# First network in units of 1, 2, 3, 4 and 6 tiles, with a re-ordered attention on fixed PSUM banks

## The chip, the core and the metric

The kernel runs on one core of a Trainium2 chip. The metric is the time of one execution on the device in microseconds (us); the median of three runs of the kernel before is 1231.76 us (1231.2 to 1231.81). TensorE does the matmuls, VectorE and ScalarE everything elementwise, SyncE starts nearly all the transfers.

## What is computed

```python
kv  = einsum('bhsd,bhse->bhde', k, v)            # 4 batches, 8 heads, 576 tokens, width 64
out = einsum('bhsd,bhde->bhse', q, kv)
x   = out / sqrt(mean(out * out, -1) + 1e-06) * g_norm     # then 2304 tokens x 512
h   = x @ w_in                                   # first network, 2048 columns
x   = (h * clip(h + 3, 0, 6) / 6) @ w_out
p   = domain_probs / domain_probs.sum(-1)        # second network, 4 experts of 1024 columns
out = sum over e of p[:, e] * (max(x @ w1[e], 0) @ w2[e])
```

The weights of the first network arrive as 64-bit floats and are converted in the kernel.

## The kernel before, in words

**Attention (L169 to L322, loop at L461).** It is cut into eight parts i, half a batch (four heads) each. Four steps belong to a part. `att_q` transposes q by a matmul with the identity into `pq` and, for the last ninth of the tokens, into `kvp`; ScalarE copies both to `qT` (L217, L219). `att_kv` multiplies k and v into `kvp` and ScalarE copies the result to `kvbd` (L234). `att_out` multiplies `qT` and `kvbd` into three PSUM tiles `po` (L247), ScalarE squares them (L253), and VectorE sums the squares into `ssq` (L256); `att_rms` makes the factor `ri` of it in six small VectorE instructions and a ScalarE square root (L277 to L286) and multiplies `po` by it into `xt` (L269, three instructions, called the scaling of part i below). `att_x` transposes `xt` back into `px` (L305), ScalarE copies that to `xh` (L315) and VectorE makes the rest `xl` (L316): `xh + xl` is the input of the first network in two terms. Round i of the loop holds `att_q` and `att_kv` of part i, `att_out` of part i-1, `att_x` of part i-2.

**First network (L329 to L396).** The 2048 columns are 16 tiles of 128. Tiles are grouped in units; for every unit the five blocks of tokens (four of 512, one of 256) are gone through, and for every block the tiles of the unit. One such step is an item: `ff_in` has 12 matmuls of 512 columns into `ph`, then ScalarE and VectorE make `gH` and `gL` (L340 to L343), and three items later `ff_out` has 12 matmuls into four PSUM banks (L357). At the end of a block in a unit, the four banks are copied to `acc` by ScalarE (first unit, L371) or added to it by VectorE (other units, L373). The first four items' `ff_in` are in a list `EARLY` and are issued inside the attention by `fill`.

**Conversion (L130 to L162).** A tile has two halves, w_in and w_out. A half takes three ScalarE instructions (L142, L143, L158) and seven of VectorE (L145 to L160), all of 512 columns. Below, the halves are numbered in the order in which they are converted. `conv(k)` asks for k steps of them in the attention, `pull` (L408) for steps by a budget during the items, and only so far ahead as L413 and L415 allow.

**Order.** The program is not executed in the order in which it is written: a list scheduler places the instructions of each engine and mixes neighbouring steps, conversions above all. The resulting order is fixed before the run. The second network (L509 on) is not touched by the change.

Of the kernel before, what the change touches and what calls it, by code (L numbers as in the profile page):

```python
# [17 lines left out]
def kernel(  # L18
# [34 lines left out]
    UNITS1 = (2, 4, 4, 6)  # L53
# [7 lines left out]
    NA = NW - UNITS1[0]  # L61
    LAG = 3
    FMAX = 3.0e38
# [18 lines left out]
    psb = ctx.enter_context(tc.tile_pool(name="psb", bufs=5, space=bass.MemoryType.PSUM))  # L82
    psc = ctx.enter_context(tc.tile_pool(name="psc", bufs=1, space=bass.MemoryType.PSUM))

    turn = [0]

    def bank_b(shape, name):
        turn[0] += 1
        pool, tag = (psc, "c") if turn[0] % 6 == 0 else (psb, "b")
        return pool.tile(shape, F32, tag=tag, name=name)  # L90
# [4 lines left out]
    three = const.tile([P, 1], F32, name="three")  # L95
    gcol = const.tile([P, 1], F32, name="gcol")
# [33 lines left out]
    def convert(n):  # L130

        u, f = ftiles[n]
        w = wp.tile([P, 2, 2, KD * P], F32R, tag=f"w{(NA + n) % NW}", name="w")
        W[u, f] = w
# [28 lines left out]


# [38 lines left out]
    def att_q(i):  # L203
# [5 lines left out]
        t["kvp"] = kvp = [bank_b([P, 2, D], "kvp") for _ in range(NP)]  # L209
        for j in range(CJ):  # L210
            for x in range(2):
                for r in range(NP):
                    to = pq[r][half[x ^ r], j, :] if j < CB else kvp[r][half[x ^ r], 1, :]
                    nc.tensor.matmul(  # L214
                        to, lhsT=t["q"][half[x], r, j, :], rhs=ident[half[x], half[x]], start=True, stop=True)
        for r in range(NP):
            nc.scalar.activation(out=qv[:, r, :, :CB], in_=pq[r].rearrange("p j s -> p s j"), func=AF.Copy)  # L217
        for r in range(NP):
            nc.scalar.activation(out=qv[:, r, :, CB], in_=kvp[r][:, 1, :], func=AF.Copy)  # L219

    def att_kv(i):
# [4 lines left out]
        for j in range(CJ):  # L226
            for x in range(2):
                for r in range(NP):
                    nc.tensor.matmul(  # L229
                        kvp[r][half[x ^ r], 0, :], lhsT=t["k"][half[x], r, j, :], rhs=t["v"][half[x], r, j, :],  # L230
                        start=(j == 0), stop=(j == CJ - 1))
        for r in range(NP):
            for x in range(2):
                nc.scalar.activation(  # L234
                    out=kvbd[i % 2][half[x ^ r], r, half[x]], in_=kvp[r][half[x ^ r], 0, :], func=AF.Copy)

    def att_out(i):
# [5 lines left out]
        for tt in banks(b):  # L243
            po = psb.tile([P, 2, NP, P], F32, tag="b", name="po")
# [14 lines left out]
    def att_rms(i):  # L259
# [4 lines left out]
        va, r0, w1_, ri = (sp.tile([P, 5, HH], F32, tag=n, name=n) for n in ("va", "r0", "nw", "ri"))  # L264

        def scale():
            for g, tt in enumerate(banks(b)):
# [8 lines left out]
        return [  # L276
            lambda: nc.vector.tensor_scalar(  # L277
                out=va, in0=ssq, scalar1=1.0 / D, scalar2=1e-6, op0=ALU.mult, op1=ALU.add),
            lambda: nc.scalar.activation(out=r0, in_=va, func=AF.Sqrt),
            lambda: nc.vector.reciprocal(out=r0, in_=r0),  # L280
            lambda: nc.vector.scalar_tensor_tensor(
                out=w1_, in0=va, scalar=FMAX, in1=r0, op0=ALU.min, op1=ALU.mult),
            lambda: nc.vector.tensor_tensor(out=w1_, in0=w1_, in1=r0, op=ALU.mult),
            lambda: nc.vector.tensor_scalar(
                out=w1_, in0=w1_, scalar1=-0.5, scalar2=1.5, op0=ALU.mult, op1=ALU.add),
            lambda: nc.vector.tensor_tensor(out=ri, in0=w1_, in1=r0, op=ALU.mult),  # L286
# [3 lines left out]
    def att_x(i):  # L290
# [8 lines left out]
        def bank(rs, o0, o1):  # L299
            px = psb.tile([P, len(rs), o1 - o0], F32, tag="b", name="px")  # L300
# [18 lines left out]
        for r in range(NP):  # L319
            bank([r], *long)  # L320
        bank(list(range(NP)), *short)
# [56 lines left out]
    EARLY = [(0, t, f) for f in range(UF[0]) for t in range(2)]  # L378
    nearly = [0]

    def fill():
        ff_in(*EARLY[nearly[0]])
        nearly[0] += 1

    def step(n):
# [39 lines left out]

    def conv(k):
        for _ in range(k):
            if cv[0] >= UF[0]:
                return
            if cv[1] is None:  # L430
                cv[1] = convert(cv[0])
            if next(cv[1], None) is None:
                cv[0], cv[1] = cv[0] + 1, None

# [3 lines left out]
    zp = psb.tile([P, DM], F32, tag="b", name="zp")  # L438
# [9 lines left out]
    load_raw()  # L448
    load_raw()
# [4 lines left out]
    nc.gpsimd.memset(three, 3.0)  # L454

# [4 lines left out]
    conv(5)  # L460
    for i in range(NHB + 2):  # L461
        if 1 <= i < NHB - 1:
            att_load(i + 1)
        if i == 4:
            nc.sync.dma_start(out=dp, in_=moe2_domain_probs.rearrange("(t p) e -> p t e", p=P))
        if i < NHB:
# [7 lines left out]
        rms = []  # L474
        if 0 <= i - 1 < NHB:
            att_out(i - 1)
            rms = att_rms(i - 1)
            rms.pop(0)()
        em = att_x(i - 2) if i >= 2 else []
        if i == NHB:  # L480
            fill()

        order = ([em[0][0]] if em else []) + rms[:1] + [x for x, _ in em[1:]]
        los = [x for _, x in em]
        order += los[:1] + rms[1:2] + los[1:2] + rms[2:4] + los[2:3] + rms[4:]
        for x in order:
            x()
    while nearly[0] < len(EARLY):
        fill()

    N3 = start[NU1 - 1, 0] + 3 * UF[NU1 - 1]
    for n in range(NI):
        step(n)
        if n == 8:
# [299 lines left out]
```

## Time and profile before

| | |
|---|---|
| median of three runs | 1231.76 us |
| the profiled execution | 1232.57 us |
| its span, first to last instruction | 1230.8 us |
| TensorE, share of the span | 99% |
| VectorE, ScalarE | 62%, 47% |
| mean granted TensorE clock | 0.993 |

The profiled execution is 0.81 us above the median, and 1.77 us of it lie outside its span. Shares are averages over the whole span: the attention takes its first 99 us, the first network goes on to about 480 us, the second takes the rest.

### The profile page before, as it was taken

What the parts mean: (1) busy time and instruction counts of PE and PEld (TensorE: products, weight loads), DVE (VectorE), ACT (ScalarE), POOL (GpSimd) and SP (SyncE); (2) the same over time, 40 slices, a digit from 0 to 9 for tenths busy, and PEclk for the clock granted to TensorE, in tenths of its full rate; (3) what the DMA queues carried; (4) which work ended last, traced back from release to release, by engine and by line L of the source; (5) the groups of instructions that cost most, each with busy time, mean ns of one, the idle gap of its engine ahead of it and who ended that gap; (6) DMA issues with size and microseconds to landing.
All of it is one profiled execution on the core that took longest, in us unless ns stands there. A gap on an engine that the chain in (4) does not pass through costs nothing.

```text
span 1230.8 us, 17514 instructions
## 1 busy us (share of the span) xinstructions
PE 1213.0 (99%) x7069; PEld 1067.4 (87%) x7069; DVE 759.0 (62%) x1457; ACT 574.6 (47%) x1146; POOL 1.6 (0%) x12
## 2 busy tenths in 40 slices
PE   7999999999999999999999999999999999999998
PEld 5778888888888889999999989999999899999997
DVE  6879993794533655565656576656565866565643
ACT  6667742542422434444444455444444644444442
POOL 0000000000000000000000000000000000000000
PEclk8999999999999999999999999999999999999999
DMA  9802320120010002222122222212222221112101
GB/s 359 258 22 69 104 86 1 52 69 1 26 44 1 1 1 69 69 69 69 69 69 69 69 86 103 69 69 69 69 69 69 73 98 64 66 66 66 68 34 52
DMA packets 60833, 87.15 MB, mean 71 GB/s; under 512 B 5200, under 2 KB 37968, under 8 KB 60752
## 3 DMA queue, kind: packets, MB, share of 16 engines
q1 hardware_dynamic: 60592, 86.03, 20.7%
q8 instruction: 55, 0.90, 0.3%
q14 instruction: 26, 0.21, 0.1%
q10 hardware_dynamic: 160, 0.00, 0.0%
HBM read 81.30 MB, written 4.72 MB: 70 GB/s over the span
## 4 chain that ended last, share of the span: by engine, by line
PE 94%; DVE 3%; DMA 2%; ACT 1%; issue 0%
PE po L636 30%; PE po L357 16%; PE qa L662 14%; PE qb L662 14%; PE ph L334 5%; PE ph L335 5%; PE ph L336 5%; PE po L247 1%; PE kvp L229 1%; DVE acc L652 1%; DMA qin<-in_q_dram 1%; DVE xs L550 1%; PE px L305 1%; DMA kin<-in_k_dram 1%; DVE st L609 1%; PE pq L214 0%
## 5 line engine op out<-in xcount | busy, mean ns | idle before, releaser
L636 PE MATMUL po<-wout,g 128*128 128x512 f32 x1728 | 402.0, 390 | 0.0
L636 PEld LDWEIGHTS po<-wout,g 128*128 128x128 f32 x1728 | 323.6, 188 | 65.4
L662 PE MATMUL qb<-xs,win 128*128 128x384 f32 x1008 | 203.4, 336 | 1.2 <-ACT us L702 1.2
L662 PE MATMUL qa<-xs,win 128*128 128x384 f32 x1008 | 203.2, 336 | 0.1
L357 PE MATMUL po<-gH,w 128*128 128x512 f32 (+1 forms) x640 | 193.7, 368 | 0.0
L549 ACT ACTIVATE wout<-raw 128x512 fp32r<-128x512 f32 x96 | 55.4, 624 | 275.4 <-PE po L636 275.4
L662 PEld LDWEIGHTS qb<-xs,win 128*128 128x128 f32 x1008 | 178.1, 188 | 3.8 <-ACT us L702 1.8
L662 PEld LDWEIGHTS qa<-xs,win 128*128 128x128 f32 x1008 | 178.2, 188 | 2.7 <-ACT st L698 0.4
L550 DVE TENSOR_TENSOR wout<-raw,wout 128x512 fp32r<-128x512 f32 x96 | 62.2, 689 | 159.0 <-ACT wout L549 159.0
L357 PEld LDWEIGHTS po<-gH,w 128*128 128x128 f32 x640 | 117.1, 189 | 20.1
L340 ACT ACTIVATE r<-ph,three 128x512 f32<-128x512 f32 (+1 forms) x80 | 51.4, 642 | 149.0 <-PE ph L336 149.0
L341 DVE SCALAR_TENSOR_TENSOR r<-r,ph 128x512 f32<-128x512 f32 (+1 forms) x80 | 50.6, 632 | 113.6 <-ACT r L340 113.5
L334 PE MATMUL ph<-xh,w 128*128 128x512 f32 (+1 forms) x320 | 118.5, 370 | 0.7 <-ACT qT L217 0.7
L335 PE MATMUL ph<-xl,w 128*128 128x512 f32 (+1 forms) x320 | 118.3, 370 | 0.0
L336 PE MATMUL ph<-xh,w 128*128 128x512 f32 (+1 forms) x320 | 118.0, 369 | 0.0
L357 PE MATMUL po<-gL,w 128*128 128x512 f32 (+1 forms) x320 | 117.8, 368 | 0.0
L691 DVE SCALAR_TENSOR_TENSOR g<-st,g 128x384 fp32r<-128x384 f32 x96 | 53.5, 558 | 81.2 <-ACT g L688 81.2
L688 ACT ACTIVATE g<-cs 128x384 fp32r<-128x384 f32 x96 | 49.8, 518 | 59.6 <-DVE cs L704 57.4
L691 DVE SCALAR_TENSOR_TENSOR g<-cs,g 128x384 fp32r<-128x384 f32 x96 | 53.3, 555 | 28.1 <-ACT g L688 28.1
L334 PEld LDWEIGHTS ph<-xh,w 128*128 128x128 f32 x320 | 60.4, 189 | 11.1 <-ACT qT L217 0.8
L335 PEld LDWEIGHTS ph<-xl,w 128*128 128x128 f32 x320 | 60.5, 189 | 10.0
L336 PEld LDWEIGHTS ph<-xh,w 128*128 128x128 f32 x320 | 60.3, 188 | 10.1
(95 smaller groups left out, 1248.8 us busy)
## 6 DMA issues: line engine op xcount, KB each, us to landing
raw<-in_moe_w_dram SPq DMA_DIRECT2D x96, 512.0 KB, 4.2
raw<-in_moe_w_in_dram SPq DMA_DIRECT2D x16, 512.0 KB, 3.8
raw<-in_moe_w_out_dram SPq DMA_DIRECT2D x16, 512.0 KB, 3.7
qin<-in_q_dram SPq DMA_DIRECT2D x8, 576.0 KB, 8.2
kin<-in_k_dram SPq DMA_DIRECT2D x8, 576.0 KB, 6.8
vin<-in_v_dram SPq DMA_DIRECT2D x8, 576.0 KB, 6.9
out_dram<-acc SPq DMA_DIRECT2D x18, 256.0 KB, 2.0
dp<-in_moe_domain_probs_dram SPq DMA_DIRECT2D x1, 36.0 KB, 4.7
```

The costliest lines, as they stand in the source:

```text
L334: nc.tensor.matmul(ph, lhsT=w[:, 0, c, :], rhs=xH[t][:, c, :], start=(c == 0), stop=False)
L335: nc.tensor.matmul(ph, lhsT=w[:, 0, c, :], rhs=xL[t][:, c, :], start=False, stop=False)
L336: nc.tensor.matmul(ph, lhsT=w[:, 1, c, :], rhs=xH[t][:, c, :], start=False, stop=(c == KD - 1))
L340: nc.scalar.activation(out=r, in_=ph, func=AF.Relu, bias=three[:, 0:1])
L341: nc.vector.scalar_tensor_tensor(out=r, in0=r, scalar=6.0, in1=ph, op0=ALU.min, op1=ALU.mult)
L357: nc.tensor.matmul(po_t[u, t][o], lhsT=lhsT, rhs=rhs, start=(f == 0 and m == 0), stop=(f == UF[u] - 1 and m == 2))
L549: nc.scalar.activation(out=dst[0], in_=src, func=AF.Copy)
L550: nc.vector.tensor_tensor(out=dst[1], in0=src, in1=dst[0].bitcast(F32), op=ALU.subtract)
L636: nc.tensor.matmul(ps[i], lhsT=lhsT, rhs=w[:, f, y], start=(j == 0 and f == 0 and m == 0), stop=(j == FP - 1 and f == 1 and m == 2))
L662: nc.tensor.matmul(bank, lhsT=w[:, wy, AOP[m], c], rhs=xs[m][:, xy, c], start=first and n == 0, stop=n == 5, skip_group_check=True)
L688: nc.scalar.activation(out=g[f][:, 0, t], in_=src, func=func)
L691: nc.vector.scalar_tensor_tensor(out=g[f][:, 1, t], in0=src, scalar=0.0, in1=g[f][:, 0, t].bitcast(F32), op0=ALU.max, op1=ALU.subtract)
```

## The change

The units become 1, 2, 3, 4 and 6 tiles, five in place of four. `EARLY` holds the first item of the first four blocks. `pull` gets a rate for each unit in place of 2100 for all. The attention's loop has nine rounds in place of ten: round i holds `att_out` of part i, `att_x` of part i-1, then `att_q` and `att_kv` of part i+1. Its loads are asked for one part further ahead, the second part's before two of the weight loads. 12 steps of conversion are asked for in the attention (one tile) in place of 22. In place of tiles that take turns in six PSUM banks there are six banks with names: `kvp` in 0 and 1, `po` in 2, 3 and 4, `px` in 5, 1 and 0. The last ninth of q is transposed first and copied to `qT` after the product of k and v. The factor `ri` is made from one square root, two reciprocals and three other small instructions: with m the mean square and s = sqrt(m)/2, it is 1 / ((m/4) / s + s), one Heron step.

```diff
-    UNITS1 = (2, 4, 4, 6)
+    UNITS1 = (1, 2, 3, 4, 6)
...
+    RATE = (4200, 3000, 2600, 2900, 0)
...
+    def bank(z, shape, name):
+        return psb.tile(shape, F32, tag=f"b{z}", name=name)
...
-        t["kvp"] = kvp = [bank_b([P, 2, D], "kvp") for _ in range(NP)]
-        for j in range(CJ):
+        t["kvp"] = kvp = [bank(r, [P, 2, D], "kvp") for r in range(NP)]
+        for j in (CB, *range(CB)):
...
-        for r in range(NP):
-            nc.scalar.activation(out=qv[:, r, :, CB], in_=kvp[r][:, 1, :], func=AF.Copy)
...
+        qv = t["qT"].rearrange("p r (s j) -> p r s j", j=CJ)
         for r in range(NP):
+            nc.scalar.activation(out=qv[:, r, :, CB], in_=kvp[r][:, 1, :], func=AF.Copy)
...
-        for tt in banks(b):
-            po = psb.tile([P, 2, NP, P], F32, tag="b", name="po")
+        for g, tt in enumerate(banks(b)):
+            po = bank(2 + g, [P, 2, NP, P], "po")
...
+            lambda: nc.scalar.activation(
+                out=s0, in_=ssq, func=AF.Sqrt, scale=0.25 / D, bias=eps4[:, 0:1]),
             lambda: nc.vector.tensor_scalar(
-                out=va, in0=ssq, scalar1=1.0 / D, scalar2=1e-6, op0=ALU.mult, op1=ALU.add),
-            lambda: nc.scalar.activation(out=r0, in_=va, func=AF.Sqrt),
-            lambda: nc.vector.reciprocal(out=r0, in_=r0),
+                out=va, in0=ssq, scalar1=0.25 / D, scalar2=0.25e-6, op0=ALU.mult, op1=ALU.add),
+            lambda: nc.vector.reciprocal(out=r0, in_=s0),
             lambda: nc.vector.scalar_tensor_tensor(
-                out=w1_, in0=va, scalar=FMAX, in1=r0, op0=ALU.min, op1=ALU.mult),
-            lambda: nc.vector.tensor_tensor(out=w1_, in0=w1_, in1=r0, op=ALU.mult),
-            lambda: nc.vector.tensor_scalar(
-                out=w1_, in0=w1_, scalar1=-0.5, scalar2=1.5, op0=ALU.mult, op1=ALU.add),
-            lambda: nc.vector.tensor_tensor(out=ri, in0=w1_, in1=r0, op=ALU.mult),
+                out=va, in0=va, scalar=FMAX, in1=r0, op0=ALU.min, op1=ALU.mult),
+            lambda: nc.vector.tensor_tensor(out=va, in0=va, in1=s0, op=ALU.add),
+            lambda: nc.vector.reciprocal(out=ri, in_=va),
...
-        for r in range(NP):
-            bank([r], *long)
-        bank(list(range(NP)), *short)
+        piece(5, [0], *long)
+        piece(1, [1], *long)
+        piece(0, list(range(NP)), *short)
...
-    EARLY = [(0, t, f) for f in range(UF[0]) for t in range(2)]
+    EARLY = [(0, t, 0) for t in range(NB - 1)]
...
-            u, t, f = items[n - LAG + 1]
-            if f < UF[u] - 1 or u == 0:
-                budget[0] = min(budget[0] + 2100, 2100)
-                pull(n)
+            rate = RATE[items[n - LAG + 1][0]]
+            budget[0] = min(budget[0] + rate, rate)
+            pull(n)
...
     load_raw()
     att_load(0)
-    load_raw()
-    load_raw()
...
     att_load(1)
-    conv(5)
-    for i in range(NHB + 2):
-        if 1 <= i < NHB - 1:
-            att_load(i + 1)
...
+    load_raw()
+    load_raw()
+    conv(6)
+    att_q(0)
+    warm(4)
+    att_kv(0)
+    for i in range(NHB + 1):
+        if i + 2 < NHB:
+            att_load(i + 2)
...
         if i < NHB:
-            att_q(i)
-            if i == 0:
-                warm(4)
-            att_kv(i)
-        conv({0: 6, 1: 11}.get(i, 0))
-        if i >= NHB - 1:
-            fill()
...
+            att_out(i)
+            rms = att_rms(i)
+        em = att_x(i - 1) if i >= 1 else []
+        his, los = [x for x, _ in em], [x for _, x in em]
+        order = rms[:2] + his[:1] + los[:1] + rms[2:4] + his[1:] + los[1:2] + rms[4:6] + los[2:] + rms[6:]
         for x in order:
             x()
+        if i + 1 < NHB:
+            att_q(i + 1)
+            att_kv(i + 1)
+        conv({0: 3, 1: 3}.get(i, 0))
+        if i in (3, 5, 7):
+            fill()
```

What this does to the order is seen at three places. In the rows, a line number is that of the kernel they belong to (the change's lines 147 to 162 are the conversion, 256 the sums of squares, 304 the transposes of `xt`, 333 to 335 `ff_in`, 356 `ff_out`, 247 `po`).

VectorE at the first sum of squares, before:

```order
L147 TENSOR_SCALAR x<-x 128x512
L160 TENSOR_TENSOR w<-r,w 128x512
L151 SCALAR_TENSOR_TENSOR a<-raw,x 128x512
L153 TENSOR_SCALAR x<-a 128x512
L155 TENSOR_TENSOR r<-r,x 128x512
L256 TENSOR_REDUCE ssq<-xt 128x8
L156 TENSOR_TENSOR r<-r,a 128x512
```

and in the change:

```order
L157 TENSOR_TENSOR r<-r,x 128x512
L158 TENSOR_TENSOR r<-r,a 128x512
L162 TENSOR_TENSOR w<-r,w 128x512
L256 TENSOR_REDUCE ssq<-xt 128x8 x2
L256 TENSOR_REDUCE ssq<-xt 64x4
L147 TENSOR_SCALAR x<-x 128x512
L279 TENSOR_SCALAR va<-ssq 128x20
L149 TENSOR_SCALAR x<-x 128x512
```

The first sum of squares stood in the third half of conversion; now it stands straight behind the first half, and the second half follows it.

TensorE around the product `po` of part 6 (the seventh), in the change; `kvp<-vin,kin` is the product of k and v of that part:

```order
L214 MATMUL kvp<-ident,qin 64x64 x2
L214 MATMUL pq<-ident,qin 64x64 x3
L227 MATMUL kvp<-vin,kin 64x64 x36
L333 MATMUL ph<-xh_112,w 128x512
L334 MATMUL ph<-xl_117,w 128x512
L335 MATMUL ph<-xh_112,w 128x512
```

and, after nine more matmuls into `ph`:

```order
L247 MATMUL po<-kvbd_108,qT 128x128 x8
L247 MATMUL po<-kvbd_108,qT 64x128 x2
L304 MATMUL px<-ident,xt 128x128 x7
```

A whole `ff_in` stands between the product of k and v and `po` in the change, here and in part 4.

TensorE at the last transposes of the attention, before:

```order
L336 MATMUL ph<-xh_115,w 128x512
L357 MATMUL po_1459<-gH,w 128x512
L357 MATMUL po_1459<-gL,w 128x512
L305 MATMUL px<-ident,xt 128x128 x4
L357 MATMUL po_1459<-gH,w 128x512
L305 MATMUL px<-ident,xt 128x128 x2
L305 MATMUL px<-ident,xt 128x64 x2
L305 MATMUL px<-ident,xt 128x128 x2
```

and in the change:

```order
L333 MATMUL ph<-xh_115,w 128x256
L334 MATMUL ph<-xl_120,w 128x256
L335 MATMUL ph<-xh_115,w 128x256
L304 MATMUL px<-ident,xt 128x128 x4
L356 MATMUL po_1436<-gH,w 128x512
L304 MATMUL px<-ident,xt 128x128 x3
L304 MATMUL px<-ident,xt 128x64 x2
L304 MATMUL px<-ident,xt 128x128
```

Ahead of the last transpose there stood 66 matmuls of 512 columns of the first network; in the change there stand 43 of them and 6 of half the width.

## Rows read from the trace of the kernel before

**Rows 1.** The page: busy shares; VectorE and granted clock in 40 slices of 30.8 us.

```profile
PE 1213.0 (99%) x7069; PEld 1067.4 (87%) x7069; DVE 759.0 (62%) x1457; ACT 574.6 (47%) x1146; POOL 1.6 (0%) x12
DVE  6879993794533655565656576656565866565643
PEclk8999999999999999999999999999999999999999
```

**Rows 2.** Waits of TensorE from 80 us to the end: us, times, longest.

```profile
PE qb L662 <- ACT us L702: 1.2, 2, 0.6
```

**Rows 3.** Stretches of the attention: length, busy (instructions), granted clock, DMA share, GB/s.

```profile
10.00:20.00 10.00, 6.29 (x154) 5.74 (x154) 6.97 (x13) 6.16 (x18) 0.00 (x0) 0.64 0.99 371
...
16.00:20.00 4.00, 2.76 (x16) 2.50 (x16) 2.34 (x5) 1.38 (x5) 0.00 (x0) 0.50 1.03 408
...
70.00:80.00 10.00, 9.34 (x115) 7.77 (x115) 4.49 (x10) 4.94 (x15) 0.00 (x0) 0.83 0.01 2
...
90.00:100.00 10.00, 10.00 (x51) 8.14 (x51) 8.87 (x21) 6.86 (x14) 0.00 (x0) 1.00 0.00 0
```

**Rows 4.** TensorE in order of time at the last transposes: start, us, line, count.

```profile
98.08 1.01 PE L305 MATMUL px<-ident,xt 128*128 128x128 f32 x6
...
103.05 0.39 PE L334 MATMUL ph<-xh,w 128*128 128x512 f32 x1
...
105.77 0.39 PE L357 MATMUL po<-gH,w 128*128 128x512 f32 x1
```

**Rows 5.** TensorE and ScalarE in order of time, first 20 us; in brackets the idle before.

```profile
10.91 1.39 PE L229 MATMUL kvp<-vin,kin 64*64 64x64 f32 x72 [3.34 <-ACT qT L219]
...
13.54 1.98 PE L214 MATMUL pq<-ident,qin 64*64 64x64 f32 x64 [1.24 <-DMA qin<-in_q_dram]
...
12.48 0.77 ACT L234 ACTIVATE kvbd<-kvp 64x64 f32<-64x64 f32 x4
```

**Rows 6.** VectorE in order of time: scalings of parts 0, 1, 5, 7 and two waits.

```profile
20.46 0.69 DVE L256 TENSOR_REDUCE ssq<-xt 128x8 f32<-128x512 f32 x1 [2.06 <-ACT xt L253]
...
27.63 1.61 DVE L269 TENSOR_TENSOR xt<-po,ri 128x512 f32<-128x512 f32 x3
...
36.71 1.60 DVE L269 TENSOR_TENSOR xt<-po,ri 128x512 f32<-128x512 f32 x3
...
71.10 1.61 DVE L269 TENSOR_TENSOR xt<-po,ri 128x512 f32<-128x512 f32 x3
77.82 0.69 DVE L341 SCALAR_TENSOR_TENSOR r<-r,ph 128x512 f32<-128x512 f32 x1 [5.11 <-ACT r L340]
...
96.51 1.61 DVE L269 TENSOR_TENSOR xt<-po,ri 128x512 f32<-128x512 f32 x3
```

**Rows 7.** One part's chain from `po` to the sums: TensorE, ScalarE, VectorE timelines.

```profile
47.12 2.63 PE L247 MATMUL po<-kvbd,qT 128*128 128x128 f32 x20
...
48.37 0.60 ACT L253 ACTIVATE xt<-po 128x512 f32<-128x512 f32 x1 [0.27 <-PE po L247]
...
49.00 1.84 DVE L256 TENSOR_REDUCE ssq<-xt 128x8 f32<-128x512 f32 x3
```

**Rows 8.** VectorE by line and shape, 0 to 95 us: count, busy us, mean ns.

```profile
L155 DVE TENSOR_TENSOR r<-r,x 128x512 f32<-128x512 f32 x7 | 4.8, 688 | 0.2
...
L145 DVE TENSOR_SCALAR x<-x 128x512 f32<-128x512 f32 x7 | 3.0, 422 | 6.5 <-ACT x L142 6.5
...
L280 DVE RECIPROCAL r<-r 128x20 f32<-128x20 f32 x8 | 2.1, 264 | 0.0
L283 DVE TENSOR_TENSOR nw<-nw,r 128x20 f32<-128x20 f32 x8 | 1.4, 175 | 0.1
```

**Rows 9.** The same, 95 to 200 us: the additions at the end of a unit's block.

```profile
L373 DVE TENSOR_TENSOR acc<-po,acc 128x512 f32<-128x512 f32 x8 | 5.1, 683 | 0.0
```

**Rows 10.** Waits of TensorE in the first 160 us: us, times, longest.

```profile
PE kvp L229 <- ACT qT L219: 4.6, 4, 3.3
```

More of the change, by code (lines that the diff above doesn't have):

```diff
@@ L60 @@
     NW = 8
-    NA = NW - UNITS1[0]
+    NA = NW - 2
     LAG = 3
+    RATE = (4200, 3000, 2600, 2900, 0)
     FMAX = 3.0e38
@@ L81 @@
     psa = ctx.enter_context(tc.tile_pool(name="psa", bufs=2, space=bass.MemoryType.PSUM))
-    psb = ctx.enter_context(tc.tile_pool(name="psb", bufs=5, space=bass.MemoryType.PSUM))
-    psc = ctx.enter_context(tc.tile_pool(name="psc", bufs=1, space=bass.MemoryType.PSUM))
+    psb = ctx.enter_context(tc.tile_pool(name="psb", bufs=1, space=bass.MemoryType.PSUM))
     turn = [0]
+    def bank(z, shape, name):
+        return psb.tile(shape, F32, tag=f"b{z}", name=name)
     def bank_b(shape, name):
         turn[0] += 1
-        pool, tag = (psc, "c") if turn[0] % 6 == 0 else (psb, "b")
-        return pool.tile(shape, F32, tag=tag, name=name)
+        return bank(turn[0] % 6, shape, name)
     for pool, n in ((padl, PADL), (padr, PADR)):
@@ L95 @@
     three = const.tile([P, 1], F32, name="three")
+    eps4 = const.tile([P, 1], F32, name="eps4")
     gcol = const.tile([P, 1], F32, name="gcol")
@@ L132, in convert @@
         u, f = ftiles[n]
-        w = wp.tile([P, 2, 2, KD * P], F32R, tag=f"w{(NA + n) % NW}", name="w")
-        W[u, f] = w
+        W[u, f] = w = wp.tile([P, 2, 2, KD * P], F32R, tag=f"w{(NA + n) % NW}", name="w")
         for h in range(2):
@@ L263, in att_rms @@
         t = st[i]
-        va, r0, w1_, ri = (sp.tile([P, 5, HH], F32, tag=n, name=n) for n in ("va", "r0", "nw", "ri"))
+        va, s0, r0, ri = (sp.tile([P, 5, HH], F32, tag=n, name=n) for n in ("va", "s0", "r0", "ri"))
         def scale():
@@ L297, in att_x, with piece @@
         em = []
-        def bank(rs, o0, o1):
-            px = psb.tile([P, len(rs), o1 - o0], F32, tag="b", name="px")
+        def piece(z, rs, o0, o1):
+            px = bank(z, [P, len(rs), o1 - o0], "px")
             for y, r in enumerate(rs):
@@ L376 @@
     NI = len(items)
-    EARLY = [(0, t, f) for f in range(UF[0]) for t in range(2)]
+    EARLY = [(0, t, 0) for t in range(NB - 1)]
     nearly = [0]
     def fill():
+        if nearly[0] == len(EARLY):
+            return
         ff_in(*EARLY[nearly[0]])
@@ L424, in pull @@
                 cv[0], cv[1] = i + 1, None
+    firsts = convert(0)
     def conv(k):
         for _ in range(k):
[L428 to L433, printed above, removed]
+            next(firsts, None)
+        cv[0] = 1
     zero = wp.tile([P, DM], mybir.dt.bfloat16, tag=f"w{NW - 1}", name="zero")
     nc.vector.memset(zero, 0.0)
-    zp = psb.tile([P, DM], F32, tag="b", name="zp")
+    zp = bank(5, [P, DM], "zp")
     def warm(k):
@@ L454 @@
     nc.gpsimd.memset(three, 3.0)
+    nc.gpsimd.memset(eps4, 0.25e-6)
     nc.scalar.activation(out=gcol, in_=three, func=AF.Sqrt)
@@ L459 @@
     att_load(1)
-    conv(5)
-    for i in range(NHB + 2):
-        if 1 <= i < NHB - 1:
-            att_load(i + 1)
-        if i == 4:
+    load_raw()
[7 more added lines that the diff above has]
+            att_load(i + 2)
+        if i == NHB - 1:
             nc.sync.dma_start(out=dp, in_=moe2_domain_probs.rearrange("(t p) e -> p t e", p=P))
+        rms = []
         if i < NHB:
-            att_q(i)
-            if i == 0:
-                warm(4)
-            att_kv(i)
-        conv({0: 6, 1: 11}.get(i, 0))
-        if i >= NHB - 1:
-            fill()
[L474 to L485, printed above, removed]
+            att_out(i)
[3 more added lines that the diff above has]
+        order = rms[:2] + his[:1] + los[:1] + rms[2:4] + his[1:] + los[1:2] + rms[4:6] + los[2:] + rms[6:]
         for x in order:
             x()
+        if i + 1 < NHB:
[4 more added lines that the diff above has]
+            fill()
     while nearly[0] < len(EARLY):
@@ L493 @@
         step(n)
-        if n == 8:
+        if n == 4 * NB:
             nc.vector.tensor_reduce(out=psum_e, in_=dp, axis=AX.X, op=ALU.add)
```

## The prediction

> **What bounds the kernel now.** I read the page first. TensorE is busy for 99% of the span and its clock stands at full speed in all slices but the first [rows 1], so only that slice and the next two or three can give anything. The list of waits says where they end: from 80 us on TensorE waits 1.2 us in all [rows 2]. The stretches say what rules before that: VectorE is busy for 9 of 10 us in most of the attention, with a hole at 70 to 80 us, and the clock is low after TensorE has idled [rows 3].
>
> So the end is set by one sum. The attention's own matmuls are the same in number before and after, and behind its last transpose TensorE has no gap. What counts is **when the last transpose ends, less the work of the first network that TensorE has done by then**. Before, the last transpose ends at 99.1 us [rows 4], with 66 matmuls of 512 columns ahead of it in the order. Twelve of them take 2.72 us, from 103.05 to 105.77 [rows 4], so one takes 0.227 us. In the change's order 43 of them and 6 of half the width stand ahead of it, worth 46. The change therefore starts with a debt of 20 x 0.227 = 4.5 us: its last transpose must end before 94.6 us to gain.
>
> **The change part by part.**
>
> *Fewer conversions in the attention.* The program asks for 12 steps in place of 22, but the scheduler takes conversions from the items and fills VectorE with them. Up to VectorE's last instruction on the attention, the order has 7 finished halves before, and 7 finished with the eighth nearly so in the change. A half has four instructions of 0.69 us and three of 0.42 us [rows 8]. The change thus does 0.8 of a half more, some 3 us, and it does them later: the first scaling comes earlier, the later ones have more between them.
>
> *Start.* Three things move the first scaling. The second q came late by 1.24 us [rows 5]; two weight loads of 512 KB are now behind it, and at the 371 GB/s of that stretch [rows 3] each is 1.4 us, so this wait goes. The product of k and v waited 3.34 us for ScalarE's copy of the last ninth of q [rows 5], part of 4.6 us in four such waits [rows 10]; the copy now comes after the product, and this goes too. And `po` of part 0 now follows at once. I take the product of k and v at 9.4 us, when by the spacing of the loads v is there, its copies done at 12.1 us (its end plus the copies' 0.77 us [rows 5] and the two of q), and `po` from there. The clock is at 1.2 GHz, half, in 16 to 20 us [rows 3], TensorE having waited at 10.91 and 13.54; I price `po` at that level, 2 us to the first bank, and get the sums of squares at 14.9 to 17.8. The second half of conversion now stands behind them and in the middle of the factor's instructions, some 3.5 us, so the first scaling starts at 22.0 us where it was at 27.63 [rows 6]: 5.6 us earlier. If the clock were full, it would start at 19.8.
>
> The Trainium skill (TensorE: Matmul & The Clock Gate, Part 1) says that the array's default is the throttled clock and that activity releases it. By that rule the low clock of rows 3 comes back wherever the change makes TensorE wait; the sum above goes by the rows, and what the rule would add later is the third case below.
>
> *Heron step.* One instruction of 0.17 us goes, another becomes a reciprocal of 0.26 us [rows 8], and the square root no longer waits for VectorE. That is 0.1 us of VectorE's work a part, 0.7 us in all; I keep it inside the sums below.
>
> *The seven rounds from scaling 0 to scaling 7.* Before, they took from 27.63 to 96.51, 68.9 us [rows 6]. For the change I add up VectorE's instructions between two scalings as the order has them, at the spacing of the rows: the three instructions of a scaling take 1.61 us in the row where 1.78 us would be the sum of their lengths, so a wide one starts 0.61 us after the last, a narrow one 0.44, a small one 0.2 to 0.3. The same way of adding gives 9.0 us for the round before from 27.63 to 36.71, which took 9.08. Beside it I follow the chain: `po` to the first sum of squares takes 1.88 us and the three sums 1.84 us [rows 7]. Round by round this gives 8.3, 9.3, 9.1, 12.2, 8.7, 10.9 and 10.8 us, 69.3 us together. The fourth is long by work: nine instructions of conversion, a fill and the probabilities' small ones stand in it beside the part's own. The sixth is long by TensorE: the product of k and v waits until the last `xl` of the part before has left bank 0 (the price of the new banks), then a whole fill of 2.72 us stands ahead of `po`, and VectorE waits about 2 us. The same pattern cost 5.11 us before, at 77.82 [rows 6], so 2 to 5 us bound it; I take 2, since the product now starts before the scaling and not after it. The seventh loses 1.5 us because ScalarE has three conversion instructions ahead of `kvbd`.
>
> *Sum.* Scaling 7 starts at 22.0 + 69.3 = 91.3 us, and the last transpose ends 3.1 us later (2.6 before [rows 4, 6], and now one piece more waits for the third instruction), at 94.4 us. Against 99.1 this is 4.7 us earlier, and 4.5 us of it pay the debt: **0.2 us gained**.
>
> *Units.* One more unit ends for each block. That is 16 additions of 0.68 us [rows 9] and four of half the width, 12.5 us of VectorE in a network of 380 us in which it is busy about 6 to 7 tenths [rows 1]; they lie beside TensorE. Adding up VectorE's order against 5.45 us for an item (24 x 0.227), it falls behind by 3 to 5 us at the end of the second unit, where blocks are half as long and additions come on top. TensorE's second `ph` buffer allows about 5.5 us, so this costs 0 to 0.7 us; I put 0.3 us. The weights of every unit are converted several items before they are used. The first unit's copies by ScalarE are as many as before.
>
> The profiled execution is 1232.57 us; -0.2 and +0.3 leave 1232.7 there. The median of the runs lies 0.81 us lower, so the forecast is **1231.9 us**.
>
> **The rivals.**
>
> *The same within 0.2%* (2.46 us, about what a measurement of this kernel can tell from no change): the sum above, with errors of 0.2 us a round.
>
> *Faster.* VectorE loses nothing in the sixth and seventh rounds (2.0 and 1.5 us) and the start runs at the full clock (2.2 us): 5.7 us at most, 1226 us. For it: VectorE has work to take in those places if the chip's order of events is a little different from mine, and the first `po` follows closer on the work before it. Against it: the order is fixed, and before it had the same hole in the same place [rows 6].
>
> *Slower.* Mechanism: the clock. Its place is the sixth round, where k and v's product, the fill and `po` stand in one chain on TensorE. At 70 to 80 us the granted clock was 0.83, after TensorE had waited [rows 3]; if the chain falls on the 1.2 GHz level, the product takes 1.3 us more, the fill 2.7 us and the first bank of `po` 1.0 us, 5 us together, and 1237 us results. It decides if TensorE idles ahead of part 6's k and v; in the fourth round the same would be covered by VectorE's work. By the Trainium skill's rule on the clock gate named above this would be expected wherever TensorE has been quiet; the rows show it at some such places and not at others.
>
> *The change does not do what it says.* That the conversions stay in the attention is in the order and so in the sum. If they were truly gone, the seven rounds would lose six halves of 3.8 us, down to a floor of some 6 us a round by the chain (0.7 us for a scaling's first instruction, 1.88 and 1.84 us [rows 7], some 1.4 us for the factor), and the conversions would fall due later; I give it no chance, since the order is fixed.
>
> **How the numbers follow.** No change to be told 0.46, faster 0.29, slower 0.25. The range takes in the faster case nearly whole and the slower one: 1226.5 to 1237.0 us.
>
> **What would show it.** First scaling near 22 us; scaling 7 near 91; rounds four, six and seven the longest; the last transpose near 94.4 with 46 matmuls' worth ahead; no TensorE wait after it but perhaps near the end of the second unit, about 160 us. The forecast is wrong if the last transpose ends below 92 or above 97 us, or if TensorE waits more than 2 us behind it.

## The result and the profile after

The changed kernel takes 1241.19 us (median of 5 runs, 1240.69 to 1242.93) where the kernel before takes 1231.59 us beside it (5 runs): a ratio of 1.008, 95% interval 1.0068 to 1.0091. It is **slower by 9.6 us**, outside the forecast's range. The profiled execution has a span of 1238.8 us, 8.0 us more than before.

The attention did not lose that time. VectorE in order of time, the scalings of parts 0, 1, 6 and 7 in the changed kernel, against [rows 6] (`...` marks rows left out, here and below):

```profile
20.85 1.60 DVE L269 TENSOR_TENSOR xt<-po,ri 128x512 f32<-128x512 f32 x3
30.29 1.60 DVE L269 TENSOR_TENSOR xt<-po,ri 128x512 f32<-128x512 f32 x3
...
79.05 1.60 DVE L269 TENSOR_TENSOR xt<-po,ri 128x512 f32<-128x512 f32 x3
89.04 1.60 DVE L269 TENSOR_TENSOR xt<-po,ri 128x512 f32<-128x512 f32 x3
```

Scaling 0 starts 6.8 us earlier than before and scaling 7 7.5 us earlier. TensorE at the last transposes and at one item behind them, against [rows 4]:

```profile
90.57 1.01 PE L304 MATMUL px<-ident,xt 128*128 128x128 f32 x6
...
98.97 0.40 PE L333 MATMUL ph<-xh,w 128*128 128x512 f32 x1
...
101.77 0.40 PE L356 MATMUL po<-gH,w 128*128 128x512 f32 x1
```

The last transpose ends at 91.6 us in place of 99.1. That is 7.5 us, of which 4.5 pay for 20 matmuls that are not yet done: 3 us gained here. Yet an item's 12 matmuls take 2.80 us (98.97 to 101.77) where they took 2.72. Waits do not explain it: from 100 us to the end the list of TensorE's waits is the same single row as in [rows 2].

```profile
PE qb L656 <- ACT us L696: 1.2, 2, 0.6
```

Nor does the clock: over the span it is 0.997 on the mean in the changed kernel, 0.993 in the kernel before. In the stretches of the attention (length, busy and instructions of TensorE, weight loads, VectorE, ScalarE, POOL, granted clock, DMA share, GB/s) it is at 0.83 where the first product waits, and at 1.00 in the sixth round and after:

```profile
10.00:20.00 10.00, 7.64 (x199) 6.74 (x190) 4.58 (x13) 6.35 (x17) 0.00 (x0) 0.83 0.98 360
...
70.00:80.00 10.00, 8.87 (x182) 7.17 (x180) 7.77 (x18) 8.41 (x18) 0.00 (x0) 1.00 0.06 16
80.00:90.00 10.00, 9.30 (x53) 7.12 (x53) 8.85 (x22) 6.87 (x17) 0.00 (x0) 1.00 0.27 93
```

What is left is the price of a matmul. TensorE by line and shape: count, busy us, mean ns of one. The records of consecutive matmuls overlap (0.39 us long, 0.227 us from start to start in [rows 4]), so a longer record is only a hint here, and the price is read further down from the starts. First the kernel before:

```profile
L636 PE MATMUL po<-wout,g 128*128 128x512 f32 x1728 | 402.0, 390 | 0.0
...
L662 PE MATMUL qa<-xs,win 128*128 128x384 f32 x1008 | 203.2, 336 | 0.1
L357 PE MATMUL po<-gH,w 128*128 128x512 f32 x512 | 168.5, 390 | 0.0
...
L357 PE MATMUL po<-gH,w 128*128 128x256 f32 x128 | 25.3, 283 | 0.0
```

And the changed kernel:

```profile
L630 PE MATMUL po<-wout,g 128*128 128x512 f32 x1728 | 400.7, 389 | 0.0
...
L656 PE MATMUL qa<-xs,win 128*128 128x384 f32 x1008 | 205.4, 339 | 0.1
L356 PE MATMUL po<-gH,w 128*128 128x512 f32 x512 | 171.5, 395 | 0.0
...
L356 PE MATMUL po<-gH,w 128*128 128x256 f32 x128 | 24.7, 279 | 0.0
```

The matmuls of 512 columns of the first network are 5 ns longer, those of 384 of the second network 3 ns, those of 256 columns 4 ns shorter; those of `wout` stay. The second network's code was not touched and its matmuls are slower too, which speaks against the units and the order. A matmul has two operands: the weights, whose loads have rows of their own in the trace (PEld), and the moving operand, named first in a row. What the slower groups have in common is where their moving operand lives in SBUF, the memory of the tiles: `xh`, `xl`, `gH`, `gL` and `xs` are allocated from its left side, `wout` from its right side. And one line of the change moves all left-side tiles, the tile of the Heron step's bias:

```diff
     three = const.tile([P, 1], F32, name="three")
+    eps4 = const.tile([P, 1], F32, name="eps4")
```

It is 4 bytes in a partition, and every left-side pool stands behind it. I take its slot to be 32 bytes; no trace shows addresses, but the first run below bears this out. The weights, allocated from the right, stay where they were. The left and right pads (`PADL, PADR = 48, 248` elements of 4 bytes), which are never read, are part of both kernels, so addresses can be moved without moving work.

### The profile page after: what moved, and what is told of

Read it like the earlier page. It is cut to its first block, busy times and chain, and to the rows that moved or that the text cites. A ratio compares the mean times of both kernels' runs of the same rounds, so it can differ in the third digit from the quotient of the medians.

```text
span 1238.8 us, 17507 instructions
## 1 busy us (share of the span) xinstructions
PE 1219.2 (98%) x7069; PEld 1065.7 (86%) x7069; DVE 765.6 (62%) x1469; ACT 574.3 (46%) x1146; POOL 1.6 (0%) x13
## 4 chain that ended last, share of the span: by engine, by line
PE 91%; DVE 5%; DMA 2%; ACT 1%; issue 0%; SPq 0%; ACTq 0%
PE po L630 30%; PE po L356 16%; PE qa L656 14%; PE qb L656 14%; PE ph L333 5%; PE ph L334 5%; PE ph L335 5%; DMA raw<-in_moe_w_out_dram 2%; PE po L247 1%; DVE acc L646 1%; DVE xs L544 1%; DVE st L603 1%; PE px L304 0%; DVE xl L315 0%; DMA qin<-in_q_dram 0%; DVE xt L269 0%
## 5 line engine op out<-in xcount | busy, mean ns | idle before, releaser
L356 PE MATMUL po<-gH,w 128*128 128x512 f32 (+1 forms) x640 | 196.2, 372 | 0.0
L335 PE MATMUL ph<-xh,w 128*128 128x512 f32 (+1 forms) x320 | 119.0, 372 | 0.0
L334 PE MATMUL ph<-xl,w 128*128 128x512 f32 (+1 forms) x320 | 119.0, 372 | 0.0
L333 PEld LDWEIGHTS ph<-xh,w 128*128 128x128 f32 x320 | 60.0, 188 | 12.7 <-DVE r L340 0.5
L334 PEld LDWEIGHTS ph<-xl,w 128*128 128x128 f32 x320 | 60.0, 188 | 11.8
L356 PEld LDWEIGHTS po<-gL,w 128*128 128x128 f32 x320 | 60.1, 188 | 11.6
```

The lines of the kernel that those rows point to most:

```text
L333: nc.tensor.matmul(ph, lhsT=w[:, 0, c, :], rhs=xH[t][:, c, :], start=(c == 0), stop=False)
L334: nc.tensor.matmul(ph, lhsT=w[:, 0, c, :], rhs=xL[t][:, c, :], start=False, stop=False)
L335: nc.tensor.matmul(ph, lhsT=w[:, 1, c, :], rhs=xH[t][:, c, :], start=False, stop=(c == KD - 1))
L356: nc.tensor.matmul(po_t[u, t][o], lhsT=lhsT, rhs=rhs, start=(f == 0 and m == 0), stop=(f == UF[u] - 1 and m == 2))
```

## The experiments

**Is it the 32 bytes?** Theory: the shift makes the wide matmuls slower, and without it the change gains. Rival: the units, the conversions or the banks slow them. Two runs, one that takes the shift from the changed kernel and one that gives it to the kernel before.

```diff
-    PADL, PADR = 48, 248
+    PADL, PADR = 40, 248
```

> The changed kernel with the left pad at 40 elements in place of 48: the 32 bytes that the new tile eps4 took are given back, and every left-side tile stands at the address that it had before the change (multiples of 128 bytes); nothing else is different. Theory (the shift of the moving operands by 32 bytes makes each wide matmul slower): 12 matmuls of the first network in 2.72 us again, and since the last transpose of the changed kernel ends some 7.5 us earlier with 20 matmuls less done ahead (4.5 us), about 1228.5 us, 3 under the kernel before. Rival (the units, the conversions or the banks make the matmuls slower): 12 in 2.80 us and about 1241 us as in the changed kernel.

Measured: 1229.74 us, ratio to the kernel before 0.9989 (0.9981 to 0.9997).

```diff
-    PADL, PADR = 48, 248
+    PADL, PADR = 56, 248
```

> The kernel before with the left pad at 56 elements in place of 48, so that accumulators, gH, gL, xh, xl and xs stand 32 bytes higher, as in the changed kernel; nothing else is different. Theory (the shift): 12 matmuls in 2.80 us in place of 2.72, about 1240 to 1243 us. Rival (units, conversions, banks): 2.72 us and 1231.6 us, no change.

Measured: 1242.24 us, ratio 1.0087 (1.0075 to 1.0099). The theory holds both ways: 8 elements of an unread pad make the whole loss and take it away. TensorE in order of time in the first of the two, and its rows by line and shape:

```profile
93.67 1.01 PE L304 MATMUL px<-ident,xt 128*128 128x128 f32 x6
...
101.97 0.39 PE L333 MATMUL ph<-xh,w 128*128 128x512 f32 x1
...
104.69 0.39 PE L356 MATMUL po<-gH,w 128*128 128x512 f32 x1
```

```profile
L656 PE MATMUL qa<-xs,win 128*128 128x384 f32 x1008 | 203.0, 336 | 0.1
L356 PE MATMUL po<-gH,w 128*128 128x512 f32 x512 | 168.6, 390 | 0.0
...
L356 PE MATMUL po<-gH,w 128*128 128x256 f32 x128 | 25.2, 283 | 0.0
```

Twelve in 2.72 us again, 390, 336 and 283 ns as before. This execution, the longest of that kernel's runs (1232.38 us), has its last transpose at 94.7 us and a span of 1230.5: 4.4 us earlier than before and 0.3 us shorter, which the debt of 4.5 us accounts for to 0.4 us.

**Which of the tiles?** One run shifts `xh`, `xl` and `xs` alone, one `gH`, `gL` and half of `acc2` (and the `x` tiles by 128 bytes).

```diff
+    padx = ctx.enter_context(tc.tile_pool(name="padx", bufs=1))
     xp = ctx.enter_context(tc.tile_pool(name="xp", bufs=1))
...
-    for pool, n in ((padl, PADL), (padr, PADR)):
+    for pool, n in ((padl, PADL), (padr, PADR), (padx, 8)):
```

> The kernel before with 8 elements of padding between the r tiles and the x tiles, so that xh, xl and xs alone stand 32 bytes higher, and gH, gL, acc and acc2 where they were. Theory (a moving operand off its multiple of 128 bytes costs some 6.6 ns in 512 columns): only the matmuls that read xh, xl and xs are slower, half of the first network's, some 5 us, and the second network's first layer, some 2.5 us: about 1239 us. If it is the engines that write gH, gL and acc which suffer, 1231.6 us.

Measured: 1241.12 us, ratio 1.0075 (1.0062 to 1.0088): 2 us more than the theory gave. From the starts of all matmuls in its trace, those of 512 columns with `xh` and `xl` follow each other after 233.5 ns on the mean and those with `gH` and `gL` after 229.5, where both were 227.1 to 227.2 in the kernel before. No other engine writes `xh` and `xl` in the first network, and the tiles that are written there did not move. So it is the reading, not the writing by other engines; but the neighbours, whose addresses did not change, were slower too.

```diff
+    padg = ctx.enter_context(tc.tile_pool(name="padg", bufs=1))
     gp = ctx.enter_context(tc.tile_pool(name="gp", bufs=4))
+    padx = ctx.enter_context(tc.tile_pool(name="padx", bufs=1))
     rp = ctx.enter_context(tc.tile_pool(name="rp", bufs=2))
...
-    for pool, n in ((padl, PADL), (padr, PADR)):
+    for pool, n in ((padl, PADL), (padr, PADR), (padg, 8), (padx, 24)):
```

> The kernel before with 8 elements of padding ahead of gH and gL and 24 behind them: gH, gL and half of acc2 stand 32 bytes higher, xh, xl and xs 128 bytes higher, so still at multiples of 128. If the cost belongs to each matmul that reads a shifted operand, half of the first network's wide matmuls (768 of 512 columns) are 6.6 ns slower and nothing else: 5 us, about 1236.5 us. If only the shift of xh, xl and xs counts (the run that shifted these alone took 1241.1 us, nearly all of the loss), about 1232 us.

Measured: 1240.5 us, ratio 1.0074 (1.006 to 1.0088), a miss for both expectations: 128 bytes, which I had taken for harmless, are not (below), so this run does not separate the two.

**Which distances?** The left pad at 64, 72, 80 and 112 elements, shifts of 64, 96, 128 and 256 bytes.

```diff
-    PADL, PADR = 48, 248
+    PADL, PADR = 64, 248
```

> The kernel before with the left pad at 64 elements, a shift of 64 bytes. If every address off a multiple of 128 bytes costs the same, as at 32 bytes, about 1241 us; if 64 bytes are enough as a multiple, 1231.6 us. The rival of units, conversions and banks expects 1231.6 us in either case.

```diff
-    PADL, PADR = 48, 248
+    PADL, PADR = 72, 248
```

> The kernel before with the left pad at 72 elements, a shift of 96 bytes. If what counts is whether the address is a multiple of 64 bytes (64 cost nothing, 32 cost 11 us), about 1242 us; if 32 is a bad phase and every other is good, 1231.5 us.

```diff
-    PADL, PADR = 48, 248
+    PADL, PADR = 80, 248
```

> The kernel before with the left pad at 80 elements, a shift of 128 bytes. If multiples of 64 or 128 bytes are free, 1231.5 us. The run that put xh, xl and xs 128 bytes higher and gH and gL 32 speaks against that (its matmuls of xh and xl were as slow as those of gH and gL, 232.4 to 233.1 ns apart): if only a multiple of 1024 is free, some 1240 us.

```diff
-    PADL, PADR = 48, 248
+    PADL, PADR = 112, 248
```

> The kernel before with the left pad at 112 elements, a shift of 256 bytes. If multiples of 64 bytes are free, 1231.5 us; if only a multiple of 512 or 1024 is, some 1240 us.

Measured: 1231.55, 1245.86, 1241.77 and 1231.61 us (the ratios are in the table below). No rule of multiples of 64, 128 or 1024 fits: 64 and 256 are free in sum, 128 is not. Multiples of 256 would fit the paces in the table, but only 0 and 256 themselves were tried.

**Own address, or distance to the weights?** Both sides shifted, then the right side alone, then the pool of the weights alone.

```diff
-    PADL, PADR = 48, 248
+    PADL, PADR = 56, 240
```

> The kernel before with the left pad at 56 and the right pad at 240 elements: left tiles (xh, xl, xs, gH, gL, acc) and right tiles (the weights w, win and wout, xt, r of the conversions) all stand 32 bytes higher, so that moving operand and weights keep their distance. If what counts is where the moving operand stands against the weights, 12 matmuls in 2.72 us and about 1231.5 us; if each operand's own address counts, at least the 1242.2 us of the run that shifted the left tiles alone.

Measured: 1233.09 us, ratio 1.001 (1.0001 to 1.002).

```diff
-    PADL, PADR = 48, 248
+    PADL, PADR = 48, 240
```

> The kernel before with the right pad at 240 elements: the weights w, win and wout and xt alone stand 32 bytes higher, the left tiles where they were. If the distance counts, as much slower as a shift of the left tiles by some odd multiple of 32 (32 gave 1242.2 us, 96 gave 1245.9 us). If only the moving operand's own address counts: w and win are weights and change nothing, but wout is moving in the second network, 1728 matmuls of 512 columns by 6.6 ns, so again some 11 us, in the second network alone (in the first it would be there by the distance): the place tells the two apart.

Measured: 1238.87 us, ratio 1.0054 (1.0039 to 1.0069). An item of the first network in the two runs, 12 matmuls in order of time, first with both sides shifted:

```profile
305.17 0.39 PE L334 MATMUL ph<-xh,w 128*128 128x512 f32 x1
...
307.89 0.39 PE L357 MATMUL po<-gH,w 128*128 128x512 f32 x1
```

Then with the right side alone, and the first matmul of its second network:

```profile
300.61 0.40 PE L334 MATMUL ph<-xh,w 128*128 128x512 f32 x1
...
303.41 0.40 PE L357 MATMUL po<-gH,w 128*128 128x512 f32 x1
...
484.35 0.34 PE L738 MATMUL qb<-xs,win 128*128 128x384 f32 x1
```

With every operand 32 bytes off, the item takes 2.72 us; with `xh` back in its old place and the weights 32 bytes off, 2.80 us. The place answers too: the second network, whose moving `wout` was shifted, starts at 484.35 us and ends with the span at 1237.1, 752.8 us. Before it began at

```profile
474.34 0.34 PE L738 MATMUL qb<-xs,win 128*128 128x384 f32 x1
```

and took 756.5. So the shifted moving operand did not slow it; its weights `g` lie in the same pool and kept their distance to it. The loss is all ahead. The last of the three narrows the right side down to one pool:

```diff
-    PADL, PADR = 48, 248
+    PADL, PADR = 48, 240
...
     wp = ctx.enter_context(tc.tile_pool(name="wp", bufs=1, side="right"))
+    padw = ctx.enter_context(tc.tile_pool(name="padw", bufs=1, side="right"))
...
-    for pool, n in ((padl, PADL), (padr, PADR)):
+    for pool, n in ((padl, PADL), (padr, PADR), (padw, 8)):
```

> The kernel before with the right pad at 240 elements and 8 elements of padding behind the pool of the weights: that pool alone (w, and with it qT, xt, raw2, wout and g2) stands 32 bytes higher; left tiles, win and the tiles of the conversions stay. If the distance of moving operand and weights counts, the first network is as slow as with all right tiles shifted (it lost 10 us up to the second network, 484.4 against 474.3 us) and the second about as before: about 1241 us. If other right-side tiles caused that loss, 1231.5 us.

Measured: 1238.89 us, ratio 1.0056 (1.0043 to 1.007), as with the whole right side. Of that pool TensorE reads only `w` in the first network: there **the distance between the moving operand and the weights** sets the price, but for the neighbours of the run with `xh`, `xl` and `xs`. The expectation for the second network, about as before, failed. Its first matmul is

```profile
481.01 0.34 PE L739 MATMUL qb<-xs,win 128*128 128x384 f32 x1
```

and it took 753.8 us in place of 756.5, although neither the distance of `xs` and `win` nor that of `wout` and `g` had changed. What made it shorter is open.

The price in one table; the third column is the mean time from the start of one 512-column matmul of the first network to the next, from all starts in the trace that are less than 300 ns apart (all but some 9 to 16 of 1536):

| shift of left tiles, of `w` (bytes) | kernel | ns from start to start | ratio to before, interval |
|---|---|---|---|
| 0, 0 | before | 227.2 | 1 |
| 0, 0 | changed, pad 40 | 227.1 | 0.9989, 0.9981 to 0.9997 |
| 32, 32 | before | 227.2 | 1.001, 1.0001 to 1.002 |
| 256, 0 | before | 227.2 | 0.9998, 0.9988 to 1.0008 |
| 64, 0 | before | 229.1 | 0.9999, 0.9987 to 1.001 |
| 128, 0 | before | 232.7 | 1.0075, 1.0058 to 1.0092 |
| 0, 32 (all right tiles) | before | 233.2 | 1.0054, 1.0039 to 1.0069 |
| 0, 32 (pool of `w`) | before | 233.2 | 1.0056, 1.0043 to 1.007 |
| 32, 0 | before | 233.3 | 1.0087, 1.0075 to 1.0099 |
| 32, 0 | changed | 233.3 | 1.008, 1.0068 to 1.0091 |
| 96, 0 | before | 233.4 | 1.0117, 1.0103 to 1.0131 |

The two operands are read at the same time: the weights of the next matmul (L335) are loaded while this one (L334) runs. Two weight loads and a matmul of the kernel before, a load taking 0.19 us of the 0.227 from one to the next:

```profile
299.85 0.19 PEld L334 LDWEIGHTS ph<-xh,w 128*128 128x128 f32 x1
300.07 0.19 PEld L335 LDWEIGHTS ph<-xl,w 128*128 128x128 f32 x1
...
300.07 0.39 PE L334 MATMUL ph<-xh,w 128*128 128x512 f32 x1
```

The Trainium skill (TensorE: Matmul & The Clock Gate, Part 2, Step-by-step: what each phase is for) gives TensorE two independent read ports, so that loading the next weights takes nothing from the running matmul. At the distances of the first four rows of the table the runs say nothing against it; at 64 bytes a matmul takes 1.9 ns more than at 0, at 32, 96 and 128 bytes 5.5 to 6.2 ns more, so by these runs the two reads are not independent at every distance. Where in the hardware they meet no run here shows.

**Where does the change's own gain come from?** At the old addresses the change is 0.11% faster, some 1.4 us. One run gives it back the old steps of the root mean square, one the old units and the old request for conversions, and one gives the kernel before the Heron step alone.

```diff
     return [
-        lambda: nc.scalar.activation(
-            out=s0, in_=ssq, func=AF.Sqrt, scale=0.25 / D, bias=eps4[:, 0:1]),
+        lambda: nc.vector.tensor_scalar(
+            out=va, in0=ssq, scalar1=1.0 / D, scalar2=1e-6, op0=ALU.mult, op1=ALU.add),
+        lambda: nc.scalar.activation(out=r0, in_=va, func=AF.Sqrt),
...
```

> The changed kernel at the old addresses (left pad 40) with the steps of the root mean square of the kernel before in place of the Heron step: the square root waits for VectorE's first step again, and there is one small VectorE step more in each of eight rounds. If this chain sets the rounds, the last transpose comes 8 x 0.3 = 2 to 4 us later than with the Heron step (1229.7 us), so 1231.5 to 1233.5 us; if the load of conversions sets them, 1229.7 us, no change.

Measured: 1233.4 us, ratio 1.0012 (1.0002 to 1.0021). Against 0.9989 with the Heron step that is 0.23%, 2.8 us. Part of it is the clock: of the 11 executions with the old steps the five longest (1233.83 us and more) have a mean granted clock of 0.994 or 0.995. Those at 0.997 and above have a median of 1231.56 us (6 of 11), with the Heron step 1229.56 us (9 of 12): about 2 us at a like clock.

```diff
-    UNITS1 = (1, 2, 3, 4, 6)
+    UNITS1 = (2, 4, 4, 6)
...
-    EARLY = [(0, t, 0) for t in range(NB - 1)]
+    EARLY = [(0, t, f) for f in range(UF[0]) for t in range(2)]
...
-        conv({0: 3, 1: 3}.get(i, 0))
+        conv({0: 6, 1: 11}.get(i, 0))
```

> The changed kernel at the old addresses (left pad 40) with the units of the kernel before (2, 4, 4 and 6 tiles), its rate of conversions and its two tiles converted within the attention; the attention's order, its banks and the Heron step stay as changed. If few conversions within the attention are what shortens it, the second tile's 12 VectorE steps of 0.69 us (8 us) come back there, less 4.5 us of first-network matmuls done ahead: some 3 us more, about 1232.5 us. If the order and the banks shorten it, about 1229 us or less.

Measured: 1229.95 us, ratio 0.9987 (0.9978 to 0.9995), the same as with the new units: the units are worth nothing here that can be told. Of the conversions this run says nothing, for the scheduler left them where they were: before the last transpose VectorE has 61 of their instructions in it and 61 with the new units.

```diff
-    PADL, PADR = 48, 248
+    PADL, PADR = 40, 248
...
+        lambda: nc.scalar.activation(
+            out=s0, in_=ssq, func=AF.Sqrt, scale=0.25 / D, bias=eps4[:, 0:1]),
...
```

> The kernel before with the Heron step alone (eps4 and its 32 bytes taken from the left pad, so all addresses as before). If the Heron step is worth the same in the old order as in the new (3.7 us), 1231.6 - 3.7 = 1227.9 us, faster than the changed kernel at the old addresses (1229.7), and the new order with its units costs 1.8 us; if it pays only in the new order, 1231.5 us.

Measured: 1230.58 us, ratio 0.9995 (0.9986 to 1.0004), no change that can be told. So the Heron step pays in the new order and the new order needs it: without it the order costs 0.12%. In which round the 2.8 us lie the profiles do not show: in single executions scaling 7 follows scaling 0 after 68.2 us in the changed kernel, 71.0 at the old addresses and 69.6 with the old steps, a scatter as large as the effect.

Part of that scatter can be read. The changed kernel and the same at the old addresses differ by 1.4 us in the fourth round, where `po` waited 1.26 us for `kvbd` at the old addresses, and by 1.5 us in the seventh. There the same 18 matmuls of `po` took 2.41 us in the changed kernel and 4.00 us at the old addresses, where the granted clock of that stretch was low:

```profile
81.12 2.41 PE L247 MATMUL po<-kvbd,qT 128*128 128x128 f32 x18 [0.19 <-ACT kvbd L234]
...
82.67 4.00 PE L247 MATMUL po<-kvbd,qT 128*128 128x128 f32 x18 [0.19 <-ACT kvbd L234]
...
80.00:90.00 10.00, 8.50 (x42) 6.61 (x41) 7.54 (x16) 6.24 (x16) 0.00 (x0) 0.83 0.35 105
```

TensorE had waited about 1.1 us for a scaling just before in both.

**A version that beats both.** Three runs with other distances (left tiles 64 bytes higher, the right side or the pool of `w` 32 bytes higher) had a second network of 753 to 754 us in place of 756. Two runs put `win` and the tiles of the conversions 64 bytes lower (16 elements behind the weights' pool), in the changed kernel at the old addresses and in the kernel before with the Heron step.

```diff
+    padw = ctx.enter_context(tc.tile_pool(name="padw", bufs=1, side="right"))
...
-    for pool, n in ((padl, PADL), (padr, PADR)):
+    for pool, n in ((padl, PADL), (padr, PADR), (padw, 16)):
```

> The changed kernel at the old addresses (left pad 40) with 16 elements of padding behind the pool of the weights: win and the tiles of the conversions stand 64 bytes lower, so that xs stands 64 bytes above its distance to win of before, and nothing else moves. The runs with another such distance of 64 or -32 had the second network in 753 us in place of 756; if that comes from xs against win (174.9 ns from matmul to matmul down to 173.9, 2016 times: 2.0 us), 1229.7 - 2 = 1227.7 us; if from the other tiles, 1229.7 us.

Measured: 1228.41 us, ratio 0.9972 (0.9961 to 0.9982): **the fastest version, 3.4 us under the kernel before by its ratio**, 2.1 of it by the pad. In the traces its second network takes 754.8 us, against 756.0 without the pad.

> The kernel before with the Heron step alone at the old addresses, and win 64 bytes lower. If both gains are there and add up, 1227.9 - 2.0 = about 1226 us; if neither, 1231.5 us.

Measured: 1229.41 us, ratio 0.9986 (0.9977 to 0.9995); 1.1 us under the same kernel without the pad; the second network takes 754.5 against 756.4 us in the traces. The intervals with and without the pad overlap, barely in the first pair and by half in the second, so both gains are estimates. That it is the distance of `xs` and `win` and not another tile's is not shown: the run with the pool of `w` shortened the second network without moving `win`.

## Why the prediction was wrong

**The step that failed** is the price in the first paragraph on the sum: "Twelve of them take 2.72 us [...] so one takes 0.227 us". It was read from the kernel before and used for the changed one, and "what counts is when the last transpose ends, less the work [...] done by then" holds only if everything behind that transpose costs the same. It did not: 12 took 2.80 us. The part on the Heron step counted its instructions and not its tile, 32 bytes ahead of every left-side pool. The price of that, from mean times between starts (changed kernel against the same at the old addresses): 1536 matmuls of 512 columns by 6.2 ns (233.3 against 227.1), 9.5 us; 384 of 256 columns by -2.8 ns (117.0, 119.8), -1.1 us; 2016 of 384 columns by 2.2 ns (176.8, 174.6), 4.4 us; 1728 with `wout` by -0.7 ns (227.1, 227.8), -1.2 us; together 11.6 us. The spans differ by 8.3 us, and the last transposes by 3.1 us the other way, 11.4 us; the two ratios differ by 0.91%, 11.2 us.

**The sum of the attention had the right shape and came out up to 2.8 us too long.** Forecast were scaling 0 at 22.0, scaling 7 at 91.3 and the last transpose at 94.4 us. The changed kernel has 20.85, 89.04 and 91.6, which is below the 92 us that the prediction itself named as a sign of being wrong. At the old addresses another execution has 21.11, 92.14 and 94.7: that this meets the forecast to 0.3 us is in part luck, since the low clock in its seventh round, 1.5 us, was not in the sum. The rounds of the changed kernel are 9.4, 8.5, 8.8, 11.6, 8.6, 11.2 and 10.0 us, with the fourth, sixth and seventh the longest, as forecast, and VectorE's wait in the sixth, priced at 2 us, was 2.41. The late second q came 0.24 us late in place of 1.24, but the third made TensorE wait 2.81 us, which the sum did not have. The forecast gain of 0.2 us was 0.11% at the old addresses, some 1.4 us, and its 1231.9 us is to be set against 1229.74.

**The parts.** That the conversions stay in the attention is what the traces show: before the last transpose VectorE spends 30.2 us on them in the changed kernel and 28.3 in the kernel before, 2 us more where 3 were forecast. The Heron step was under-sized: 0.7 us of VectorE's work was forecast, the runs give 2.8 us in this order, about 2 at a like clock, and nothing that can be told in the old one. The lag of 0.3 us at the end of the second unit did not come; TensorE has no wait in the first network.

**The rivals.** "Slower" came out, but not by its mechanism: the clock stood at 1.00 in the sixth round. In the changed kernel the low clock showed only at 10 to 30 us. The Trainium skill's rule (TensorE: Matmul & The Clock Gate, Part 1), by which the throttled clock is the default, would have allowed it at TensorE's later waits too; the trace of the changed kernel does not show it there, that of the same kernel at the old addresses does in the seventh round, at 80 to 90 us. So the mechanism did show in one execution, in a round that lasted 1.5 us longer, and it is not what made the loss. "Faster" by 5.7 us did not come at the old addresses either.

## What to carry to other kernels

When every matmul gets a few nanoseconds longer, with no wait and at full clock, compare the durations by line and shape before and after, also in code that was not touched, and then the addresses: a tile of 4 bytes at the head of the pools moves everything behind it. In a kernel bound by TensorE, one unread pad is worth a try on either side of the memory; here the distance of moving operand and weights is worth up to 1.2%, more than any edit of the order that was tried. Read the granted clock of each stretch before comparing single executions: it alone moved one by 1.5 us. Reserve the slot, or take it from a pad, before timing an edit that adds a tile.

## What was not expected of the hardware

- The distance between the SBUF addresses of moving operand and weights, given here as the shift against the kernel before, changes the pace of 512-column matmuls between 227.2 ns (0 and 256 bytes) and 233.4 ns (96 bytes).
- The sign depends on the width: at 32 bytes, 256 columns are faster (117.0 against 119.8 ns), 512 and 384 slower.
- At 64 bytes the pace of the 512 columns is 229.1 ns, 2 more than at 0, but the second network is shorter (753.2 against 756.5 us), and the sum is no change.
- A matmul's pace also depends on its neighbours: `gH` and `gL` at their old distance took 229.5 ns between items whose `xh` and `xl` were shifted. Why is open. So is the rest of 0.1% when both sides were shifted, and why the matmuls with `wout` go from 227.8 to 227.1 ns when only left-side tiles have moved.
- After like waits of 1.1 us, `po` of part 7 ran at a granted clock of 1.00 in one execution and at 0.83 in another (stretch of 80 to 90 us): 2.41 us and 4.00 us for the same 18 matmuls.
